# Joining two table products of a half group, with a new order of the pieces and new PSUM pair names, in a kernel of windowed attention beside a long convolution

## The chip, the core and the metric

The kernel runs on one core of one Trainium2 chip. The core has a matrix engine (PE, with its weight loads listed as PEld), a vector engine (DVE), a scalar engine (ACT), a general engine (POOL) and a queue engine (SP) that issues nearly all transfers (DMAs). Each engine works through its own instructions in the order in which the program emitted them; engines wait for each other by semaphores. PE writes only to PSUM, a small memory that DVE and ACT read.

The metric is device time in microseconds, from first to last instruction. Before the change the median of three runs is 782.46 us (779.48 to 783.68).

## What is computed

Two independent results are placed side by side, each 2048 x 576 numbers.

```
qkv = x @ wqkv                       # 2048 x 576 by 576 x 1728, 32 heads of 18
s   = q k^T / sqrt(18), keys 0..255 back only
a   = softmax(s) v, heads joined, @ wo

P   = exp(dt*A * l)                  # complex, per channel d, 128 states, l = 0..2047
K   = Re sum_n C_n P_n(l) dt*B_n     # the taps of a filter, 576 x 2048
b   = causal convolution of u with K, + u * Dskip
out = concat(a, b)
```

## The kernel before

**Four stages.** `front` loads weights and x and starts the projections. `tables` computes the projections q, k and v, the filter taps K and the first step of the transforms of u and K. `first` is short and ends the tables while attention starts. `rest` runs attention, the convolution in the transform domain, and at its end the product with wo. Attention works on 16 items (4 column blocks of 512 queries by 4 groups of 8 heads).

**The taps.** The 576 channels are 18 groups of 32, each two half groups of 16 channels. A half group c has a phase tile `fr` (sine and cosine, 128 x 2 x 512), an exponential table `mg` that stays in PSUM (128 x 1024), their products `Q` made by DVE in `t_q` (L595), and a table `m` made by POOL (`t_prod`, L579) and summed by DVE (`t_add`, L590). `t_taps` (L607) multiplies `m` and `Q` on PE.

**The order is written out by hand.** Each stage has a string in `PLAN` (L85). A letter is one step of a stream, and a letter with a digit is the next due follow-up of that kind of that stream. The emission order only fixes, for each engine, the order of its own instructions. Letters that matter here:

| letter | step | follow-ups |
|---|---|---|
| P | a third of a product of the projections, on PE (L417) | P1 P2 the high and low half of q and k, P5 v to SBUF, P4 P6 stores |
| G | angles of a group or a phase of a half group, on PE | G1 G2, G5 G6: ACT, then DVE |
| N, R | sine and A (ACT, POOL); product and sum (POOL, DVE) | |
| M | alternately `mg` on PE (M1: exp on ACT) and `t_q` on DVE | M1 |
| X | taps of a half group or transform of a group, on PE | X1 X5 ACT, X2 DVE, X4 store |
| U | first transform of u | U1 ACT, U2 DVE, U4 store |
| s | smax: scores of 64 queries for their row maximum, 16 to an item, then a transposition, on PE (L888) | s2: the maximum on DVE (L940), s6, s4 |
| a | score: one of 10 blocks of scores of an item, on PE (L962) | a1: exp on ACT (L1000) |
| v | pv: probabilities by v, 10 to an item, on PE (L1004) | v1: ACT |
| n | norm on DVE | n3 POOL, n1 ACT, n6 POOL, n4 the store of the item |
| c, d, e | spectra, inverse, last transform of the convolution, on PE | ACT, DVE, POOL, stores |
| f, k, L, y | loads by SP: convolution results, spectra, items, and the normed items for wo | |
| w | half of the product with wo for 128 rows, on PE (L1132) | w1 ACT, w4 store |

An item's row maxima go back into its Q tile by four small transfers (L933) before its first score step. The third item is loaded at the start of `first`, into memory that the projections leave.

**PSUM.** Three pairs of banks, called ring0 to ring2, serve all steps but the projections and pv. `SLOTS` (L134) names, one digit per tile, which pair each tile takes in the order of PE's steps. A step that takes a pair waits until the tile that had it before has been read by its follow-up. Projections have two banks of their own (`pp`), which pv (`po`) takes over.

**The end.** The wo product runs over 4 blocks c of 512 rows, 4 times 128 rows each, two halves h. `wo_in` (L1118) loads block c in two parts u of 256 rows with 8 transfers each, into the same tile for all c; part u of block c needs the stores of the items 4c to 4c+3 and waits for the wo steps that still read these columns.

Of the kernel before, what the change touches and what calls it, by code (L numbers as in the profile page):

```python
# [15 lines left out]
OP = mybir.AluOpType  # L16
# [13 lines left out]
HC = GC // 2  # L30
# [12 lines left out]
def constants():  # L43
# [23 lines left out]
    for nm, v in mult.items():  # L67
# [16 lines left out]

PLAN = {  # L85
    "front":
        "AAAVCACAAAAAVAVVV1CV1CAVAVAAVCAV1ACCVCACCVVV1VV1CVCACBBPABV1CCPV1BV1CPCPP1PVP2PP4CPAPP1PP2BPCP1P4BVP"
        "CP",
    "tables":
        "GMGPGPG5G6G1PM1GG5GP2G2PGG6P4NMMG5P1G6G5G1P2PPNM1PP4G6P1GPG2UNRP2G1MMRXPP1M1P2P4X1RMGG5NG2PRMPGP1G5X"  # L90
        "X1M1XG6X5GP2RG6PMX2RNRUPGU2PMG1UP1PG5G2M1RGNU1XXX1UG6P2MPX1G5U2RG6PX4MU1XP4RRPM1X4PXPGX5X2P1GNMUMP2P"
        "1PX1PG1RXP2M1P4PG2X1GP4PG5MUNRU1PG5G6MX4U2G6XP1U4RPRM1PPPGX5P4P2P1NMRGPP2MNXXX4G5X2G1P1P4PM1X1G6G2P4"
        "P2U4X1XMGPMGX5G5RP1PG6M1PP2X2PP4NRPP4RPMP1MG1PP2PM1UX4PP1XGRX1NP4XG2PP2GX1MG5UX4G5MPG6U2G6X4P4RU1U4R"
        "P1M1X4XX2PPXMRNU4P2GPX5P1X1MNRP2PXG1G2P4PGM1X1PG5PPXP5X4GPPP5RX5UMG5G6PG6UPPNU1UX2MRRPP4U2M1U4UU2XPP"
        "5MMRX1PGP5P6UG1U1PM1PPPG2P5UX4NRU1PMPMGM1XPP5PX1U2RU4G5P5GG5PPG6RMGXG6PP5PRX2NP6NP4PPG1MG2XPPGX5PRM1"
        "UP1G5P2P1MMGX1M1G5G6P2G6X4RXX4PPX1NXPPGP1X2PX5MGP4X4XG1RRP2MPX1PG5PNM1RG2G6XP1GX1PG5P1MMM1XG6X2P2X4P"
# [32 lines left out]
        "e4wewwn6w1e1yfww1wn4w1w4www1w4wwe4feeywe1w1ww4w4yw4wwe1we4w1ww1w4www1w4w1e4w4w4",
}  # L130

SLOTS = (  # L134
    "0122021210220122120112011211020210220101210201012021020012120012010210121000212102201221020110012201"
    "2011021012010201021120101201201201020201210210212012120210210120120021021102010212012212012012012012"
    "0120120210202021021021021020120120102102102020120120120121002102101202102012102102120121021201201201"
    "2012012010210210210210210210210120120120120120120120120120121021021012012012021021021021201201201201"
    "2101201201210210201210210210212012021020121020120120120210210210212010212012012012012021021012102102"
    "0102102102012012012010210210120120120210210201201201201210210201201201201201201201201201202102102101"  # L140
    "2012012010210210120120121021021021021021020120120120210120120102102102102102120120120120121200201201"
    "202010210210200210210212012"
)


# [9 lines left out]
class Kernel:  # L155
# [439 lines left out]
    def t_q(self, c):  # L595
        nc, tt = self.nc, self.nc.vector.tensor_tensor
        f = self.fr.pop(c)
        sn, cs = (f[:, i].rearrange("p (c m) -> p c m", m=32) for i in range(2))
        m = self.mg.pop(c)
        Q = self.Q[c] = self.p["Qp"].tile([128, HC, 2, 64], F32, name="Q")  # L600
        tt(Q[:, :, 0, 32:64], cs, m[:, :, 32:64], op=OP.mult)
        tt(Q[:, :, 0, 0:32], cs[:, :, ::-1], m[:, :, 0:32], op=OP.mult)
        tt(Q[:, :, 1, 32:64], sn, m[:, :, 32:64], op=OP.mult)
        nc.vector.scalar_tensor_tensor(Q[:, :, 1, 0:32], sn[:, :, ::-1], -1.0, m[:, :, 0:32],
                                       op0=OP.mult, op1=OP.mult)

# [666 lines left out]
```

## Time and profile before

| what | value |
|---|---|
| median of 3 runs | 782.46 us |
| all runs | 783.68, 779.48, 782.46 us |
| span of the profiled execution | 784.5 us (no other time of this execution is recorded) |
| mean granted clock of PE | 0.963 |
| instructions in the span | 29499 |
| moved by DMA | 150.67 MB |

The profile is one execution. Its page gives the busy time of each engine and the chain of work that ended last. Further views of the same trace group instructions by line, list the waits, cut the span into windows, or list instructions in order of time. In a row of the timeline the columns are start, duration, engine, line, operation, output and inputs, count, and in brackets the idle time before it with the engine and line that ended it. In a row of windows they are the length, the busy time of each engine with its count, then the granted clock of PE (1.00 is full), the DMA share and GB/s.

### The profile page before, as it was taken

The page shows a single profiled execution, that of the slowest core. Times are in us where ns is not written, and L with a number is a line of the kernel's source. Part 1 is how long each engine was busy: PE and PEld are TensorE (multiplying, and loading weights), DVE is VectorE, ACT ScalarE, POOL GpSimd, SP SyncE. Part 2 cuts the span into 40 slices and gives each one's busy share as a digit, 9 for nine tenths or more (in the row PEclk, how much of TensorE's full clock was granted, in tenths as well). Part 3 has the DMA queues.
Part 4 walks back from the last instruction along what each step waited for, and adds up shares of the span by engine and source line. Part 5 has one row for each costly group of instructions (what it writes and reads, how often), then busy time and mean ns, then how long its engine had stood idle before and what let it go on. Part 6 is the DMA issues. An engine that isn't in the chain of part 4 may idle for free.

```text
span 784.5 us, 29499 instructions
## 1 busy us (share of the span) xinstructions
PE 693.0 (88%) x12956; PEld 410.8 (52%) x12956; DVE 588.2 (75%) x779; ACT 534.3 (68%) x709; POOL 417.3 (53%) x309
## 2 busy tenths in 40 slices
PE   3786878998989989997789999989989998999997
PEld 2532444565545654665544555544555554557775
DVE  5998789998998897988777888876888586852100
ACT  2369577787887777773458677775877876786622
POOL 2245867987688666866007574451553444546120
PEclk9979799999999999996999999998999999899999
DMA  8998055738247537889578777676866786555786
GB/s 309 342 215 204 7 133 149 159 83 216 51 120 182 133 70 175 230 183 277 113 238 279 247 240 231 207 243 166 245 185 203 240 256 207 170 163 159 205 258 187
DMA packets 215904, 150.67 MB, mean 192 GB/s; under 512 B 103530, under 2 KB 195818, under 8 KB 215520
## 3 DMA queue, kind: packets, MB, share of 16 engines
q1 hardware_dynamic: 214160, 146.28, 66.0%
q0 software_dynamic: 1616, 2.52, 1.1%
q8 instruction: 101, 1.65, 0.8%
q14 instruction: 27, 0.22, 0.1%
HBM read 83.50 MB, written 65.11 MB: 189 GB/s over the span
## 4 chain that ended last, share of the span: by engine, by line
PE 55%; DVE 17%; ACT 15%; issue 6%; DMA 4%; SPq 1%; POOL 0%; ACTq 0%; DVEq 0%
PE po L1020 9%; PE pp L204 9%; PE ring L204 7%; PE ring L906 5%; DVE m L940 5%; PE ring L752 4%; PE ring L982 4%; PE ring L615 4%; PE ring L718 4%; PE ring L505 2%; DMA wraw<-in_wr_dram 2%; DVE amx L192 2%; PE ring L815 2%; ACT raw L1000 2%; DVE wl L372 2%
## 5 line engine op out<-in xcount | busy, mean ns | idle before, releaser
L940 DVE TENSOR_REDUCE m<-ring 128x2 f32<-128x640 f32 (+4 forms) x256 | 190.8, 779 | 66.0 <-PE ring L914 58.2
L586 POOL TENSOR_TENSOR m<-A,tr 128x1024 f32<-128x1024 f32 x72 | 141.5, 1983 | 52.6 <-DVE m L592 43.5
L1000 ACT ACTIVATE P<-ring,esc 128x1024 f32<-128x1024 f32 (+2 forms) x86 | 90.0, 1060 | 37.1 <-PE ring L995 32.7
L1000 ACT ACTIVATE raw<-ring,esc 128x1024 f32<-128x1024 f32 (+2 forms) x74 | 77.2, 1061 | 19.4 <-PE ring L995 18.8
L734 POOL TENSOR_TENSOR t<-X 128x768 f32<-128x768 f32 x24 | 46.7, 1944 | 76.1 <-ACT X L726 75.6
L1063 POOL TENSOR_TENSOR oh<-osb,oh 128x1024 f16<-128x1024 f32 x16 | 34.1, 2133 | 59.5 <-ACT oh L1059 42.9
L914 PE MATMUL ring<-sm,idb 64*64 64x128 bf16 x896 | 56.1, 224 | 3.3 <-issue 3.1
L204 PE MATMUL pp<-xh,wh 128*128 128x512 f16 x180 | 48.1, 397 | 10.0 <-DVE qst L453 5.0
L204 PEld LDWEIGHTS <-wh 128*128 128x128 f16 x324 | 30.7, 99 | 49.1 <-issue 11.7
L615 PE MATMUL ring<-Q,m 128*32 128x64 f32 x2304 | 42.9, 231 | 12.8 <-ACT fa L511 4.1
L1055 POOL TENSOR_TENSOR osb<-osb,T 128x1024 f32<-128x1024 f32 x16 | 38.6, 2410 | 25.8 <-DVE T L1050 23.8
L592 DVE TENSOR_TENSOR m<-m,m 128x1024 f32<-128x1024 f32 x36 | 51.6, 1432 | 0.7 <-POOL m L586 0.6
L615 PEld LDWEIGHTS ring<-Q,m 128*32 128x32 f32 x2304 | 36.9, 117 | 27.2 <-ACT mab L547 5.5
L906 PEld LDWEIGHTS <-raw 54*64 54x64 f16 x704 | 28.6, 108 | 41.1 <-issue 37.7
L740 POOL TENSOR_TENSOR Y<-t,t 128x384 f32<-128x384 f32 x24 | 24.7, 1029 | 46.1 <-DVE t L734 33.8
L906 PE MATMUL ring<-K,raw 54*64 54x320 f16 (+4 forms) x576 | 44.8, 308 | 4.5 <-ACT raw L1000 0.8
L204 PE MATMUL pp<-xh,wl 128*128 128x512 f16 x180 | 48.0, 400 | 0.6 <-DVE wl L372 0.6
L567 POOL TENSOR_TENSOR tr<-tr,mab 128x768 f32<-128x768 f32 x18 | 33.3, 1850 | 28.4 <-ACT tr L562 28.4
L726 ACT ACTIVATE X<-ring 128x768 f32<-128x768 f32 x48 | 36.7, 812 | 14.3 <-PE ring L718 8.1
L995 PE MATMUL ring<-tm,idb 64*64 64x256 bf16 (+2 forms) x640 | 45.0, 257 | 0.0
L982 PEld LDWEIGHTS <-K 55*64 55x64 f16 x1280 | 28.8, 108 | 26.7 <-issue 22.7
L752 PE MATMUL ring<-Y,i 32*64 32x192 f32 x768 | 38.7, 336 | 3.3 <-issue 2.3
(171 smaller groups left out, 1725.1 us busy)
## 6 DMA issues: line engine op xcount, KB each, us to landing
gk<-kst SPq DMA_DIRECT2D x36, 256.0 KB
gx<-ust SPq DMA_DIRECT2D x16, 576.0 KB
xk<-gx SPq DMA_DIRECT2D x24, 384.0 KB
xk<-gk SPq DMA_DIRECT2D x24, 384.0 KB
h<-ho SPq DMA_DIRECT2D x48, 192.0 KB
hp<-h SPq DMA_DIRECT2D x24, 384.0 KB
K<-kz SPq DMA_DIRECT2D x14, 512.0 KB
raw<-qz SPq DMA_DIRECT2D x11, 512.0 KB
```

The costliest lines, as they stand in the source:

```text
L204: self.nc.tensor.matmul(ps, u, v, start=(i == 0), stop=(i == len(ops) - 1))
L586: tt(m[part], A[:, ch, a0:a0 + 8].unsqueeze(3).to_broadcast(sh), tr[:, ch, part, 0:8].unsqueeze(2).to_broadcast(sh), op=OP.mult)
L592: self.nc.vector.tensor_tensor(m[0], m[0], m[1], op=OP.add)
L615: nc.tensor.matmul(kp[32 * st:32 * st + 32, j, :], m[:, ch, 32 * term:32 * term + 32], Q[:, ch, term, :], start=(term == 0), stop=(term == ...
L734: mul(ts[i], X[:, :, :, :192].rearrange("p i s j -> p s i j"), X[:, i, :, 192:].unsqueeze(2).to_broadcast(sh), op=OP.mult)
L752: nc.tensor.matmul(ps[64 * (b % 2):64 * (b % 2) + 64, b // 2, 192 * s:192 * s + 192], self.i1[32 * b:32 * b + 32, t, o:o + 64], Y[32 * b:3 ...
L906: nc.tensor.matmul(ps[z:z + 64, b, :n], d["Q"][rr, 2 * b + pp, 64 * qb:64 * qb + 64], d["K"][rr, 2 * b + pp, k0:k1], start=True, stop=Fals ...
L914: nc.tensor.matmul(out, self.idb[rr], self.sm[rr], start=False, stop=True, skip_group_check=True)
L940: self.nc.vector.tensor_reduce(out, x, axis=AX.X, op=OP.max)
L982: nc.tensor.matmul(ps[z:z + 64, b, off:off + w], d["K"][rr, 2 * b + pp, kc:kc + 64], d["Q"][rr, 2 * b + pp, q0:q0 + w], start=(k == 0), st ...
L1000: nc.scalar.activation(P[:, :, lo:hi], ps[:, :, lo:hi], AF.Exp, scale=self.esc)
L1020: nc.tensor.matmul(po[32 * p:32 * p + 32, z, q0:q0 + w], V[64 * z:64 * z + 64, kb * 76 + 19 * p:kb * 76 + 19 * p + 32], P[p % 2][64 * z:64 ...
```

## The change

In `t_q` two products of `mg[32:64]`, with cosine and with sine, become one instruction. It reads the sine and cosine tiles in reversed order as one operand of 16 x 2 x 32 elements and repeats the table along that middle dimension. The number of elements written is the same. The other two products keep their own instructions.

```
-        tt(Q[:, :, 0, 32:64], cs, m[:, :, 32:64], op=OP.mult)
+        tt(Q[:, :, :, 32:64], f.rearrange("p i (c m) -> p c i m", m=32)[:, :, ::-1],
+           m[:, :, 32:64].unsqueeze(2).to_broadcast([128, HC, 2, 32]), op=OP.mult)
         tt(Q[:, :, 0, 0:32], cs[:, :, ::-1], m[:, :, 0:32], op=OP.mult)
-        tt(Q[:, :, 1, 32:64], sn, m[:, :, 32:64], op=OP.mult)
         nc.vector.scalar_tensor_tensor(Q[:, :, 1, 0:32], sn[:, :, ::-1], -1.0, m[:, :, 0:32],
                                        op0=OP.mult, op1=OP.mult)
```

All strings of `PLAN` and `SLOTS` are replaced. Every step and follow-up occurs as often as before in the whole program, and `front` differs in two places (the store of the constant rows goes before two stores of q on SP, and the high half of the third projection product goes behind the last conversion of weights on ACT). The start of `tables`, the string `first` and the end of `rest`:

```
     "tables":
-        "GMGPGPG5G6G1PM1GG5GP2G2PGG6P4NMMG5P1G6G5G1P2PPNM1PP4G6P1GPG2UNRP2G1MMRXPP1M1P2P4X1RMGG5NG2PRMPGP1G5X"
+        "GGG1G2PP1P2P2P4ZMM1G5G6GPPG5GG6P4NMPNRGGG5G6GG5G6G1PP1P2P4PPPPG2NURRMM1MG1P1P2PMG2GG5XG6M1RX1MMM1XGN"
...
     "first":
-        "s6X5s4sX2s2sX4s2RMsss2M1saaRs2Xa1ssa1s2X1MRXs2X1sXX4saas2aX5sas2sX2X4sa1sa1s2vX4s2vs2a1ss2X4s2s2ss2s"
-        "s2aavsa1sssa1s",
+        "Xss2s2X1XX5X2aa1ss2sas2ss2aaa1a1sss2s2a1vsss2vs2vaa1sss6sss2ss2s2s2ss2aaa1sa1s2vsaa1s2ss2ss2X4X4",
...
-        "e4wewwn6w1e1yfww1wn4w1w4www1w4wwe4feeywe1w1ww4w4yw4wwe1we4w1ww1w4www1w4w1e4w4w4",
+        "e1ywww1www4w4ee4yww1w4ww1www1w4w4www1e1e4e4www4w1w4",
```

Counted from the strings, with the steps on PE behind `front` numbered from 0 (1014 in both):

| PE step | number before | number after |
|---|---|---|
| first taps | 18 | 21 |
| first smax of item 0 | 323 | 309 |
| last projection step | 320 | 348 |
| last transform of K (end of the tables) | 355 | 354 |
| first score of item 0 | 348 | 355 |
| first smax of item 2 | 374 | 371 |
| first spectra | 405 | 401 |
| last pv | 990 | 990 |

The number of PE steps from a tile to the next tile in the same pair, counted over all tiles of a stage:

| stage | 1 or 2 steps, before | after | 3 steps, before | after |
|---|---|---|---|---|
| tables | 32 | 42 | 42 | 32 |
| first | 10 | 6 | 16 | 16 |
| rest | 46 | 63 | 144 | 128 |

Two neighbouring PE steps of one kind in `rest`: smax behind smax 42 times before and 57 after, score behind score 19 and 34, score behind smax or smax behind score 161 and 123.

Behind the last pv, PE has the same steps in both orders: 12 wo halves and 3 last transforms, then the 8 wo halves of block 3. On SP, the second part of block 2 (8 loads) and one convolution load stand ahead of the store of the last item in both. Before the change one output store of wo and one of the convolution (two transfers) stand ahead of these 8 loads, behind the store of item 14; after it none does. On ACT, item 14's conversion to half precision moves behind item 15's copy out of PSUM, and item 15's conversion stands behind two wo outputs there instead of one.

More of the change, by code (lines that the diff above doesn't have):

```diff
@@ L92 @@
[L92 to L96, printed above, removed]
@@ new lines @@
+        "4PX5P4P1MP4P4MM1PP2GP1X2G5X4X4PPG6NUU1RP2U2X4PPU4PP4P4MMGRRP1P2G1M1PU4G2XX1PGG5P1XP4X1MG6GG5PPP1MM1P"
+        "2PNG6NRXX5RP2PPPP1X2XX4X4X4PMMP2X1P4RPRM1PP5UMUU2PPUU1P5PXX1GGG5G6GG5PG6PG1G2P5PPNPPPPRRXNX2XX5U4X4X"
+        "1UP5U1MRUM1U2P5URU1U2PPPMGP5MG1PU4U4M1XPX1G2GG5MPPGPG6G5G6PPNP5RP5XRX5MP6GP6P6PPPM1NG1RX2PPXX1RPMMP1"
+        "P4G2P1P4P2P4P2GXM1X1MPPX4G5G6GG5G6NRRMRPX4XX2PM1PPUP1P2MNXPX5MP1X1P2GG1M1GPP4RP4G2PP1XX1PP6GMG5G5G6G"
+        "6P2XMX4X2X5M1NRRNPPP1UU2P4P4MUPP2XX1PRRU1UX4U2GPMG1G2U1M1MMXM1P1P2PX1GG5X4G6NX4RGG5PG6PPRMXNP4X2UPPX"
@@ new lines @@
+        "5P1P1UP2GG1RPPU4U1P4U2PRP5UMM1X4X4P2G2XP4XX1X1MNGPG5G6MPPM1GP5PPG5PG6NP6XPP5RPRZZX2X5PXX1PPX4PRP5GG1"
+        "PMNGPG5P4MRPP5PG2RPM1PP5PG6P5GXPMG5G6X1XX2PUPX5U4U2P6MP5U1RRRP6UP6GM1NPPPP1G1PPXX1U4PMMG2XM1X1UP2PU1"
+        "NP1MGG5X4U2MX4X4GPPP2PM1PPG6G5G6XRRNMP1RP4P4P1XP2X5U4X1GG1X2UUU1RPU2MP2M1PGPG2XMP1P2G5P4X1GMG6G5G6X4"
+        "PX4M1PNP4RRMPPXX2NP1X5P2ZRRGU4XX1X4X4G1PMZPG2PPP1P2P4GM1P4MG5NGG5G6G6RPRP1PUUMU1XU2RPPP2M1X1NNXMX2PR"
+        "UPX5UP1XU4U1U2GUG1P2G2PMPM1P5X1X4PPUMU4U1U4U2U4GGG5G5P5G6PG6PRRMP6M1XMX4P4PPPX1XX5PX4X2sss2ss2sss2s2"
@@ L129 @@
[L129 removed]
+        "vaa1ssss2vs2avss2s2vs4aa1a1aa1ksvss2kaa1ss2s2cc1sLLss6svv1s2sss2s2lsss2s2s2c2aa1svvsc6s2c3sks2kcs2ss"
+        "2c1aava1alkskka1a1Laa1lvcs2c6vvc2nc1aa1aa1svvs4aa1dc3d1c2ss2n3s2sc6vvs2ksaaLs2v1a1Lda1Lnad1a1sc3vcc1"
+        "c6n3s2ss6sas2ss2a1aa1ss2vsass2a1s2vksaas4a1s2a1sava1s2ss2aa1svvs2ss2aaaa1a1ss2vac2c3svvks2a1a1aa1sss"
+        "2s2n1n6cc1sds2sc2LLLvd4v1dd1s2ss6kLssd4d1svs2s2c6c3s2kcc1sc6s2dsd4s2avd1a1ss2aa1aa1c2ssn1n6s2s2vvaa1"
@@ new lines @@
+        "ss2ss2s4sks2kcc1savvc3c6ss2s2a1aa1c2c3kdd4d1savvkss2s2a1aa1d4aLa1dd1Lnvss2vv1n4cc1sLLLd4s6asc2aa1a1v"
+        "kss2s2ss2ks4kan3va1ss2ss2sss2aa1svs2s2sasa1s2s2vn4vssd4s2s2aa1n1ss2c6c3vsss2ss2s2css6Lc1Laac6avva1a1"
+        "a1Lssvaa1ns2vss2as2sa1s2sn6v1dss2s2vc2vss2ad1a1sn3aa1s2aa1c3sn1s2vals4avvn4a1vnsn3svs2s2n6a1ss2kcc1k"
+        "kss2aa1c6ad4ss2vaaa1sls2a1a1vvLLfc2aa1sffeLs2c3ss6Le1e4fkkaa1sss2ss2s2csv1c1c6vs4ss2s2sas2vvsss2s2a1"
+        "n1dsss2d1vs2Lsas2da1anc2d1slva1avLLs2aa1a1svs2ss2asLvvs2a1ala1saa1s2n3sss6kvn4s2ss2sn6v1cs2c1sls2ala"
@@ new lines @@
+        "1vsaa1s2ss2vn1sass2s2ss2vlkss2a1ss2llaa1vad4ffa1see1svs2s2ss4ass2s2a1Lc3c2vaa1kc6n6cc1dc3dd4d1d1snaa"
+        "1LLLvs2ss6ss2vsssn4vvv1s2ss2s2s2d4aa1ss2as4vss2ya1aa1vasvss2s2aa1a1aa1vsn3ss2vss2s2aa1ee1kc2ss2ss2va"
+        "nn1ca1c6c1avkn4saLa1ss2a1as2a1vss6aac3c6LLLn6svs2vkkLa1a1ssas2s2skv1vn3s2c2a1avsa1ss2cc1as2da1asnvd1"
+        "vsc3s2c6n4c2c3n3s4a1asla1s2lvs2sssvvn1n6s2s2LLsaa1s2s2ss2e4e4aa1ss2avss2La1ala1vvv1sss6ssks2s2aa1s2v"
+        "aa1d4sksvvs2s2sssn1s2Lan6n4s2a1vsvss2s2s2aca1s4svc1c6aa1svs2aa1s2fsfdsd1s2s2ac2asvs2a1ss2d4vva1ss6aa"
@@ new lines @@
+        "v1a1LLdLa1nd1lsas2vss2aa1a1vssss2s2s2ac3a1vss2scc1s2ss2aaka1va1sn3nd4s2ydd1d4ee1ss2sc2vvs4avn1a1s2ss"
+        "2kc6kLLsn4s2cc1Lss2vass2a1aka1n6aa1ss2vvc3Lss6ac2a1ss2dd1n3ss2v1d4sss2s2c6cc1ss2avsaa1sks2s2vffaka1a"
+        "1aa1kn1c3svc2ss2vsfs2s2see1aa1s2ss2dss2ss2e4ld1vn6cc6c3c1lss4ass2s2vaann3a1a1a1d4LLfLc2aa1vess6n4vLs"
+        "d4e1aa1s2ss2llvvsdv1vad1a1s2ss2kcss2vd4c6c1sss2c3s2dd1aasla1va1c2ss2ks2vssks2c6c3ls2kcc1ac6a1ss2kvvs"
+        "n1s2aa1cc2c3vc1c6sss2dsd1s2s2fdsls6s4ad4d1kfe4a1waaa1a1d4ww1wwaaLw1vd4a1a1c2c3kcvc1n6vaaa1w4wwa1aaff"
@@ L143 @@
+    "0120102102102102102120102102102012010210210210201201201202102120120120210210201201201201201201201202"
+    "1021021021201021021021021021020120121021021012012102102102102102120120121021021021201012012012012012"
+    "102102102102102102101021010"
 )
```

52 lines of the change are left out of this document (13 added, 39 removed).

## The prediction

> **What bounds the kernel now.** I read the engines' busy time and the chain's shares on the page first, then a table of windows that cuts the span where its character changes.
>
> ```profile
> PE 693.0 (88%) x12956; PEld 410.8 (52%) x12956; DVE 588.2 (75%) x779; ACT 534.3 (68%) x709; POOL 417.3 (53%) x309
> PE 55%; DVE 17%; ACT 15%; issue 6%; DMA 4%; SPq 1%; POOL 0%; ACTq 0%; DVEq 0%
> 0.00:60.00 60.00, 38.03 (x142) 20.87 (x143) 49.17 (x53) 24.20 (x32) 17.34 (x22) 0.91 0.91 287
> 60.00:100.00 40.00, 30.15 (x247) 14.57 (x247) 32.55 (x47) 30.96 (x49) 29.41 (x25) 0.83 0.46 109
> 100.00:355.00 255.00, 231.84 (x3233) 137.64 (x3231) 225.47 (x307) 198.62 (x319) 190.79 (x148) 0.99 0.60 145
> 355.00:405.00 50.00, 38.27 (x985) 26.18 (x989) 40.85 (x66) 20.62 (x29) 13.71 (x13) 0.83 0.75 209
> 405.00:700.00 295.00, 274.87 (x7280) 154.16 (x7272) 228.62 (x296) 222.82 (x241) 143.21 (x92) 0.98 0.73 221
> 700.00:784.50 84.50, 79.79 (x1082) 57.39 (x1080) 11.51 (x14) 37.04 (x44) 22.88 (x13) 1.00 0.64 196
> ```
>
> The chain is mostly PE, with DVE and ACT in turns: no one engine is late, they hand PSUM pairs to each other. In the tables (100 to 355) PE has 91% and DVE 88%, so DVE time saved there can show. In attention with the convolution (405 to 700) PE has 93%, 20.1 us idle in all, and DVE 77%. The loosest place is the transition, 355 to 405: PE is idle for 11.7 of 50 us and its clock is 0.83. The end is PE alone.
>
> **Joined product.** Two instructions of 512 elements become one of 1024, 36 times.
>
> ```profile
> L601 DVE TENSOR_TENSOR Q<-fr,ring 128x512 f32<-128x512 f32 x36 | 24.5, 680 | 7.6 <-ACT ring L527 4.9 <-PE ring L615 2.0 <-ACT fr L557 0.7
> L603 DVE TENSOR_TENSOR Q<-fr,ring 128x512 f32<-128x512 f32 x36 | 24.4, 679 | 0.0
> 350.35 0.68 DVE L602 TENSOR_TENSOR Q<-fr,ring 128x512 f32<-128x512 f32 x1
> 350.94 0.68 DVE L603 TENSOR_TENSOR Q<-fr,ring 128x512 f32<-128x512 f32 x1
> 351.54 0.67 DVE L604 SCALAR_TENSOR_TENSOR Q<-fr,ring 128x512 f32<-128x512 f32 x1
> 353.19 1.22 DVE L592 TENSOR_TENSOR m<-m,m 128x1024 f32<-128x1024 f32 x1
> 354.33 0.68 DVE L514 TENSOR_TENSOR fr<-ring,fr 128x512 f32<-128x512 f32 x1
> ```
>
> Each lasts 0.68 us, but the next starts 0.60 us on (350.35, 350.94, 351.54). A product of 1024 lasts 1.22 us and the next starts after 1.14. By starts the pair falls from 1.20 to 1.14, 0.06 x 36 = 2.2 us; by durations from 1.36 to 1.22, 0.14 x 36 = 5.0 us. The trace has no product with a repeated, reversed operand of this shape; a loss is excluded by L602, which reads reversed at the same 0.68, and by the means of 679 and 680 ns over 36, which show that this PSUM operand meets no contention. So 0 to 5.0. I take the starts, nearest to what a queue without gaps pays, times DVE's 88%: **-2 us**.
>
> [...]
>
> **The start of the tables.** Here PE waits longest, 4.12 us for the first taps.
>
> ```profile
> 78.01 1.94 PE L615 MATMUL ring<-Q,m 128*32 128x64 f32 x64 [4.12 <-ACT fa L511]
> ```
>
> The new order has two more projection thirds ahead of these taps, but also one more low half of q (0.6 us of DVE by the start spacing) ahead of the first phases, on which sine, POOL's product and the taps hang. What is filled is work moved up, what is late is the chain: 0, with -2 and +1 as bounds.
>
> **The transition.** Before, all projections end first and then smax of item 0 runs as a block, with DVE's maxima behind it.
>
> ```profile
> 340.00:345.00 5.00, 4.12 (x84) 2.73 (x85) 1.89 (x3) 4.67 (x9) 3.74 (x5) 1.00 0.78 170
> 360.00:365.00 5.00, 3.82 (x80) 2.67 (x80) 4.92 (x12) 0.18 (x1) 4.76 (x7) 0.50 0.92 216
> 365.00:370.00 5.00, 4.42 (x102) 3.14 (x103) 4.35 (x6) 0.06 (x1) 3.08 (x4) 0.50 0.98 375
> 353.63 0.65 PE L204 MATMUL pp<-wh,xl 128*128 128x288 f16 x4
> 361.51 7.83 DVE L940 TENSOR_REDUCE m<-ring 128x2 f32<-128x128 f32 x14
> 361.65 0.32 PE L906 MATMUL ring<-raw 54*64 54x128 f16 x4 [1.10 <-DVE Q L604]
> 365.21 0.68 SPq L882 DMA_DIRECT2D V<-vd  x1
> Q<-qz SPq DMA_DIRECT2D x5, 512.0 KB
> 393.61 0.22 PE L906 MATMUL ring<-K,Q 54*64 54x64 f16 x4
> ```
>
> DVE has 3.1 us free in 340 to 345 and is full at 361.51, where 14 maxima take 7.83 us while ACT does nothing. The new order starts smax 14 steps earlier and ends the projections 28 steps later, so maxima and projections run beside each other. What can be won is bounded by DVE: its idle 9.15 us of 355 to 405. Against it stands the third item's load. It needs memory of the projections, so it goes out behind the last of them. Before, it was issued by 365.89 and wanted at 393.61, 27.7 us later; the new order leaves 23 PE steps instead of 54. Three transfers of at most 0.5 MB each at the stage's 209 GB/s are 7 us and their issues 2 (3 x 0.68); 23 steps of maxima at 0.56 us are 13. It fits, and where it does not, smax waits in PE's queue and all scores behind it. I put that at up to 4. So -9 to +4, and I take a third of the gain: **-3 us**.
>
> **The pairs of PSUM in `rest`.** This speaks against the change.
>
> ```profile
> L940 DVE TENSOR_REDUCE m<-ring 128x2 f32<-128x640 f32 x224 | 176.4, 821 | 60.0 <-PE ring L914 58.2
> L1000 ACT ACTIVATE P<-ring,esc 128x1024 f32<-128x1024 f32 x72 | 79.4, 1114 | 27.0 <-PE ring L995 26.4
> 443.59 0.33 PE L906 MATMUL ring<-K,raw 54*64 54x320 f16 x4 [0.32 <-ACT ho L759]
> 443.87 0.33 PE L906 MATMUL ring<-K,raw 54*64 54x320 f16 x4
> 458.71 0.33 PE L982 MATMUL ring<-raw,K 55*64 55x320 f16 x4 [0.26 <-ACT P L1000]
> ```
>
> A smax occupies PE for 0.28 us (443.59 to 443.87), its maximum DVE for 0.82, an exp ACT for 1.11. A pair named again with one step between leaves PE short by about 0.8 us where that step is a smax (1.11 less 0.33), with two by 0.45. One-step cases go from 46 to 63, two-step cases from 144 to 128: +13.6 and -7.2, a net 6.4 us if all were of this kind. On the same scale the order before would lose 37 + 65 = 102, while PE's measured idle is 20.1, a fifth: many of these steps are long. Behind the wait stand all further smax, score and pv steps in PE's queue, and so DVE and ACT. Between a fifth (1.3) and all (6.4) I take **+3 us**, since scores and smax now come in blocks (164 like neighbours against 122) and DVE idles while ACT has a block.
>
> **The end.**
>
> ```profile
> 737.37 3.24 PE po L1020 x121
> 749.01 13.35 PE ring L204 x108
> 763.12 3.33 DMA oh<-od
> 767.21 13.40 PE ring L204 x108
> 748.78 2.12 POOL L1063 TENSOR_TENSOR oh<-osb,oh 128x1024 f16<-128x1024 f32 x1 [1.49 <-ACT oh L1059]
> 755.15 1.48 SPq L1068 DMA_DIRECT2D od<-oh  x4
> 760.65 0.93 SPq L1129 DMA_DIRECT2D oh<-od  x1
> 762.77 2.86 PE L815 MATMUL ring<-hp,i 128*64 128x384 f32 x16
> ```
>
> Item 15 is ready at 750.90, its store goes out at 755.15, its loads from 760.65; PE ends its other work at 765.63 and waits until 767.21, 1.58 us. In the new order two stores less stand before, ACT's two moves cost item 15 0.6 us, and its 8 loads wait for two wo rows of block 2 (4 halves of 1.68) behind 4 others and two transforms: 740.61 + 6.7 + 2.9 + 6.7 = 756.9, 3.7 before 760.65. The wait goes, and PE alone is late next, with the same steps: **-1.5 us** (0 if the store still goes out as late).
>
> **Sum.** -2 - 3 + 0 + 3 - 1.5 = -3.5 on 784.5, 781.0 for the profiled execution. That one lies 2.04 over the median of 782.46; I keep the difference: **779.0 us**.
>
> **Rivals.**
>
> *A full transition.* All 9 us of DVE's idle go, the pairs cost 1.3 instead of 3, the rest as summed: -2 - 9 + 1.3 - 1.5 = -11.2, 771. For it: at 360 to 370 PE is busy 8.24 us at clock 0.50, so filled gaps would also double its pace (up to 4 us of PE time). Against it: DVE is full there. [...]
>
> *Pairs asked for too soon (the other side).* All 6.4 us in `rest`, and the same in the tables, where cases of one step or none go from 32 to 42.
>
> ```profile
> L511 ACT ACTIVATE fr<-ring 128x512 int32<-128x512 f32 x36 | 21.5, 598 | 11.9 <-PE ring L505 9.4 <-POOL wi L338 1.7 <-DVE Q L604 0.6
> ```
>
> A phase tile holds its pair for 0.60 on ACT and 0.68 on DVE; ten such cases cost up to 10 x 1.28 less 5 for a step between, some 8. With the transition at nothing: -2 + 6.4 + 8 - 1.5 = +10.9, 793. It decides when the extra waits pass the 6.5 us of gains; in the tables DVE, not PE, would have to be left without work.
>
> *The change does nothing that counts.* DVE waits 7.6 us ahead of L601 anyway, so the saved 2.2 end as longer waits, and order against order cancels: 782.5, within 2.
>
> **Chances.** 0.5% is 3.9 us, about what a measurement of this kernel can tell from no change: 778.5 and 786.4 are the bounds. The forecast (775.5 to 782.5) 0.45, of it 0.18 below the bound; full transition (768 to 776) 0.25; pairs (785 to 796) 0.25, of it 0.04 within; nothing 0.05. Faster 0.43, same 0.36, slower 0.21. The range leaves out the ends of both rivals: 770 to 791. The likeliest case's own range is 775.5 to 782.5.
>
> **What would show it.** Right: L601 at some 1.22 us, DVE 2 to 5 us less busy; maxima from L940 beside projections, and less PE idle than 11.7 us where smax of items 0 and 1 runs; attention with somewhat more PE idle than 20.1 us; no DMA wait ahead of the last 13.4 us. Wrong: smax of item 2 waiting for its load, idle PE in the tables behind L511 or L514, or clock dips at new places.

## The result, and the profile after

| | before | after |
|---|---|---|
| median of the runs side by side, us | 783.07 (779.48 to 786.34) | 792.68 (788.60 to 796.93) |
| span of the profiled execution | 784.5 | 791.2 |

The ratio of the times is 1.0138, with a 95% interval from 1.0093 to 1.0183: the change costs 7 to 14 us. 779.0 was forecast, with 770 to 791 as the range. A median here and below is over all runs of a kernel, while a ratio leaves out runs more than 1.5% above the kernel's fastest, so that for e4, e5 and e6 the two don't quite match.

The page of the changed kernel, first the busy time of the engines, then the shares of the chain:

```profile
PE 691.7 (87%) x12956; PEld 403.3 (51%) x12956; DVE 581.9 (74%) x743; ACT 533.2 (67%) x709; POOL 417.4 (53%) x309
PE 45%; DVE 22%; DMA 11%; ACT 11%; issue 6%; SPq 3%; POOL 1%; DVEq 0%; ACTq 0%
```

DVE works 6.3 us less and no engine works noticeably more, and yet the span is 6.7 us longer. In the chain PE falls from 55 to 45%, while DMA rises from 4 to 11% and SP's queue from 1 to 3%. Time is lost in waits, and transfers are among them. But a transfer can stand on the chain with its whole length where PE waited for its last part alone: the load `K<-kz` takes 7.08 us of the chain from 402.11 on, and PE waits 0.34 us for it.

The table of windows, with the same columns as before and the same cuts:

```profile
0.00:60.00 60.00, 37.78 (x143) 20.96 (x144) 49.12 (x54) 23.07 (x30) 16.21 (x22) 0.94 0.95 297
60.00:100.00 40.00, 29.92 (x232) 13.51 (x231) 29.92 (x38) 28.20 (x44) 23.64 (x20) 0.70 0.35 88
100.00:355.00 255.00, 227.16 (x3181) 133.08 (x3180) 225.17 (x279) 197.70 (x317) 196.42 (x152) 0.99 0.60 145
355.00:405.00 50.00, 41.17 (x1021) 26.56 (x1027) 38.94 (x63) 23.35 (x35) 15.38 (x13) 0.94 0.83 205
405.00:700.00 295.00, 269.09 (x7102) 146.98 (x7087) 226.37 (x299) 214.96 (x233) 139.30 (x90) 0.98 0.70 214
700.00:791.20 91.20, 86.61 (x1293) 62.23 (x1290) 12.41 (x14) 45.97 (x53) 26.47 (x14) 1.00 0.69 208
```

Three rows differ. From 60 to 100 PE's clock is 0.70 instead of 0.83. From 355 to 405 PE idles 8.8 us instead of 11.7 and runs at 0.94 instead of 0.83: the transition became denser, as meant. From 405 to 700 PE idles 25.9 us instead of 20.1, and 1293 matmuls instead of 1082 are left at 700.

**The joined product,** from the groups by line with shapes kept apart:

```profile
L601 DVE TENSOR_TENSOR Q<-fr,ring 128x1024 f32<-128x1024 f32 x36 | 43.6, 1212 | 4.9 <-ACT ring L527 4.1 <-ACT fr L557 0.8
L603 DVE TENSOR_TENSOR Q<-fr,ring 128x512 f32<-128x512 f32 x36 | 24.4, 677 | 0.0
```

One instruction of 1212 ns stands for two of 680, as forecast. For the 36 pairs the rows give 24.5 + 24.4 - 43.6 = 5.3 us of DVE, where the prediction's durations gave 5.0. That this would shorten the kernel the runs below don't show.

**The start of the tables.** The timeline of PE, the first taps; then SP's queue and one row of ACT ahead of them:

```profile
87.42 1.93 PE L615 MATMUL ring<-Q,m 128*32 128x64 f32 x64 [0.55 <-DVE fa L514]
```
```profile
48.21 3.25 SPq L412 DMA_DIRECT2D kz<-ones  x1
51.55 2.48 SPq L466 DMA_DIRECT2D qz<-qst  x1
54.13 2.26 SPq L467 DMA_DIRECT2D qz<-qst  x1
56.44 2.41 SPq L466 DMA_DIRECT2D qz<-qst  x1
58.90 2.56 SPq L467 DMA_DIRECT2D qz<-qst  x1
```
```profile
64.89 0.60 ACT L450 ACTIVATE qst<-pp 128x512 f16<-128x512 f32 x1 [6.70 <-DMA qz<-qst]
```

The first taps start at 87.42 instead of 78.01. The store of the constant rows (L412, 2 x 1280 KB) now goes out ahead of the first stores of q. Behind it the next four issues take SP over 2 us each, where these stores of q took 0.31 to 0.39 before. The staging tile of q comes free late, ACT stands 6.70 us in front of it, and the sines behind it in ACT's queue (L556) start at 68.71 instead of 62.58.

**The start of attention.** SP's queue and one row of PE:

```profile
385.59 5.62 SPq L639 DMA_DIRECT2D gk<-kst  x2
391.32 2.07 SPq L776 DMA_DIRECT2D w<-in_c_w_dram  x1
393.58 0.82 SPq L776 DMA_DIRECT2D i<-in_c_i_dram  x2
394.50 2.49 SPq L933 DMA_DIRECT2D raw<-m  x4
397.10 0.53 SPq L706 DMA_DIRECT2D xk<-gx  x1
```
```profile
402.14 1.08 PE L982 MATMUL ring<-raw 55*64 55x64 f16 x8 [3.16 <-DMA raw<-m]
```

The row maxima of item 1 go back into its Q tile at 394.50, behind the last stores of K's transform and 2 MB of constants; they land when PE has waited 3.16 us for them. Before, the only wait of a score step for such a store, in the whole execution, is one of 0.4 us:

```profile
PE ring L982 <- DMA raw<-m: 0.4, 1, 0.4
```

**The end.** The last pieces of the chain:

```profile
744.56 3.27 PE po L1020 x118
747.82 6.97 PE ring L204 x56
754.79 2.73 PE ring L815 x16
757.52 13.83 PE ring L204 x112
771.35 1.44 PE ring L815 x8
772.79 11.93 PE ring L204 x97
```

No transfer stands ahead of the last block any more: the 1.58 us of before are gone. PE wasn't idle for all of them. Two rows of its timeline before, at the start of this block:

```profile
766.49 0.42 PE L204 MATMUL ring<-woh,oh 128*128 128x288 f16 x2 [0.51 <-DMA oh<-od]
767.21 0.28 PE L204 MATMUL ring<-woh,oh 128*128 128x288 f16 x1 [0.30 <-issue]
```

Its idle time there was 0.81 us, 0.51 of it for the load; in the rest it worked on four matmuls of the block. From the last pv's end to the span's end it is 43.4 us instead of 43.9.

### The profile page after: what moved, and what is told of

The parts are those of the page before. It is cut to its first block, busy times and chain, and to the rows that moved or that the text cites. A ratio compares the mean times of both kernels' runs of the same rounds, so it can differ in the third digit from the quotient of the medians.

```text
span 791.2 us, 29495 instructions
## 1 busy us (share of the span) xinstructions
PE 691.7 (87%) x12956; PEld 403.3 (51%) x12956; DVE 581.9 (74%) x743; ACT 533.2 (67%) x709; POOL 417.4 (53%) x309
## 4 chain that ended last, share of the span: by engine, by line
PE 45%; DVE 22%; DMA 11%; ACT 11%; issue 6%; SPq 3%; POOL 1%; DVEq 0%; ACTq 0%
PE ring L204 7%; PE po L1020 7%; PE pp L204 6%; DVE m L940 5%; PE ring L752 4%; PE ring L982 4%; PE ring L906 4%; PE ring L718 3%; DMA K<-kz 3%; DVE m L592 3%; DVE Q L601 2%; PE ring L815 2%; DMA wraw<-in_wr_dram 2%; DVE amx L192 2%; PE ring L505 2%
## 5 line engine op out<-in xcount | busy, mean ns | idle before, releaser
L940 DVE TENSOR_REDUCE m<-ring 128x2 f32<-128x640 f32 (+4 forms) x256 | 190.1, 779 | 67.7 <-PE ring L914 64.6
L592 DVE TENSOR_TENSOR m<-m,m 128x1024 f32<-128x1024 f32 x36 | 53.7, 1492 | 5.5 <-POOL m L586 5.4
L914 PE MATMUL ring<-sm,idb 64*64 64x128 bf16 x896 | 53.5, 220 | 4.4 <-issue 4.4
L615 PE MATMUL ring<-Q,m 128*32 128x64 f32 x2304 | 41.1, 226 | 8.1 <-DVE Q L604 2.6
L726 ACT ACTIVATE X<-ring 128x768 f32<-128x768 f32 x48 | 36.7, 809 | 16.9 <-PE ring L718 11.7
L601 DVE TENSOR_TENSOR Q<-fr,ring 128x1024 f32<-128x1024 f32 x36 | 43.6, 1212 | 4.9 <-ACT ring L527 4.1
L615 PEld LDWEIGHTS ring<-Q,m 128*32 128x32 f32 x2304 | 35.4, 113 | 21.1 <-issue 6.6
L906 PEld LDWEIGHTS <-raw 54*64 54x64 f16 x704 | 25.7, 106 | 39.9 <-issue 36.1
```

The source lines that it names most:

```text
L592: self.nc.vector.tensor_tensor(m[0], m[0], m[1], op=OP.add)
L601: tt(Q[:, :, :, 32:64], f.rearrange("p i (c m) -> p c i m", m=32)[:, :, ::-1], m[:, :, 32:64].unsqueeze(2).to_broadcast([128, HC, 2, 32]), ...
L615: nc.tensor.matmul(kp[32 * st:32 * st + 32, j, :], m[:, ch, 32 * term:32 * term + 32], Q[:, ch, term, :], start=(term == 0), stop=(term == ...
L906: nc.tensor.matmul(ps[z:z + 64, b, :n], d["Q"][rr, 2 * b + pp, 64 * qb:64 * qb + 64], d["K"][rr, 2 * b + pp, k0:k1], start=True, stop=Fals ...
L914: nc.tensor.matmul(out, self.idb[rr], self.sm[rr], start=False, stop=True, skip_group_check=True)
L940: self.nc.vector.tensor_reduce(out, x, axis=AX.X, op=OP.max)
```

## The experiments

Theories were A (the front costs the time), B and later C (the order inside attention does), D (the tables and the transition do, later D2, in e8 called E: the transfers at the start of attention), F (the names of the pairs), G (blocks of smax steps wait for DVE's maxima), H (the order of the engines' steps, whatever the resource) and I (transfers in general). A gain or loss below is the ratio to the kernel before times 782.5 us, with its 95% interval; the change itself stands at +10.8 (7.3 to 14.3).

**The parts that are easily parted: front and product.** e1 and e2 exchange one string (below for e1; for e2 it is the other way round), e3 and e4 the product, by the diff of the change above.

```
     "front":
-        "AAACVAAACAAAVAACVV1CV1VAVAAAACVV1AVV1CVCVCV1VCCCAPCCBBV1VVBCAACV1V1VVPBCCPPPP1PP2P4CPPP1P2P4PBCCBPP1"
-        "PP",
+        "AAAVCACAAAAAVAVVV1CV1CAVAVAAVCAV1ACCVCACCVVV1VV1CVCACBBPABV1CCPV1BV1CPCPP1PVP2PP4CPAPP1PP2BPCP1P4BVP"
+        "CP",
```

> The changed kernel with the stage string front of the kernel before: the store of the constant rows goes behind the first two stores of q again, and the high half of the third projection product goes ahead of the last weight conversion. Theory A (the front costs the time): ACT's wait of 6.7 us for a q staging tile goes, the first taps start at 78 to 80 us instead of 87.4, and the total falls by 5 to 9 us against the changed kernel, to 784 to 788. Theory B (the order in attention costs the time): the first taps come as early, but the tables are bound by PE and DVE and no more than 2 us of it reach the end; the total stays at 790 to 793.

> The kernel before with the stage string front of the changed one, nothing else. Theory A (the front costs the time): first taps at 84 to 88 us instead of 78.0 and a total of 788 to 792, 5 to 9 us over the kernel before. Theory B (attention costs it): first taps late by some us, total within 2 us of the kernel before.

> The kernel before with the joined product alone, old order and old pairs. By the forecast: one instruction of 1.21 us in 36 places for two, DVE 5 to 6 us less busy, total 2 us less (0 to 5), 778 to 783. If DVE's saved time only lengthens its waits: within 1 us of the kernel before.

> The changed kernel with the two products apart as before: new order and new pairs alone. By the forecast 2 us more than the changed kernel (0 to 5), 793 to 797. If DVE's time in the tables is not what sets their end: within 1 us of the changed kernel.

| | time, us | against before |
|---|---|---|
| e1, new with old front | 792.11 | +8.8 (5.2 to 12.4) |
| e2, old with new front | 780.95 | -1.4 (-3.8 to +1.0) |
| e3, old with joined product | 781.52 | -0.1 (-2.7 to +2.6) |
| e4, new with two products | 797.85 | +11.7 (7.1 to 16.3) |

In e1 the timeline shows the first taps early again:

```profile
81.06 1.93 PE L615 MATMUL ring<-Q,m 128*32 128x64 f32 x64 [0.55 <-DVE fa L514]
```

6.4 us earlier, and the time doesn't follow. Theory A falls. In e2 the new front alone leaves the first taps at 78.15: it takes the new order of the tables behind it to make the late store felt. The other 3 us of the delay (81.06 against 78.01) come with the new order of the tables whatever the front. The joined product brings nothing that these runs can tell from no change: its 2 us lie within e3's interval, and e4's lies over the change's, but overlaps it.

**Splices.** The two orders hold the same steps, so one can be followed up to a point and then what is left be done in the other's order, with the other's pairs. The code of the change is kept throughout. The first lines that differ in e6, where the old order takes over at the start of `rest`:

```
-        "vaa1ssss2vs2avss2s2vs4aa1a1aa1ksvss2kaa1ss2s2cc1sLLss6svv1s2sss2s2lsss2s2s2c2aa1svvsc6s2c3sks2kcs2ss"
+        "as4a1vakLsvssksvLvksa1sks2vvv1as2ala1s2s2s2sas2s2aa1svcvsaa1a1as6snsasvc1cac6a1s4s2ss2va1ks2a1kLas2c"
...
```

> The changed kernel's code with the order of before up to the end of the stage first, and from there the pieces that are left in the new order with their new pairs. Theory C (the order inside attention costs the time): 788 to 793, as the changed kernel. Theory D (the loss lies in the tables and the transition): 779 to 784, as the kernel before.

> The reverse: the new order up to the end of the stage first, then the pieces that are left in the old order with their old pairs. Theory C (attention's order costs the time): the forecast's gain of the transition shows, 776 to 782. Theory D (tables and transition): 787 to 793.

> The new order up to score step 6 of item 6, somewhat under half of attention, then the old order. If the loss falls at one place at the start of attention (late transfers of item 1's maxima and of item 3's load at 394 to 409 us): 788 to 793, the whole loss. If it accrues with the pairs over all of attention: about half of it, 784 to 787. If it comes late: 778 to 783.

> The new order up to score step 4 of item 2 (some 430 us), then the old order with its pairs: the new order's start of attention alone, with its transfers of 394 to 410 us. Theory D2 (the transfers at the start of attention cost most): 789 to 794. Theory G (the many short waits between 410 and 545 us): 783 to 788, as the run that changed back at the start of the stage rest (786.2).

> The old order up to score step 6 of item 6, then the new order with its pairs: the reverse of e7. If all of the loss lies in the first part of attention, as e7 (whole loss) says: 778 to 783. If the second part costs as well: 785 to 790.

| | time, us | against before |
|---|---|---|
| e5, old, new from `rest` on | 793.49 | +9.8 (2.3 to 17.2) |
| e6, new, old from `rest` on | 786.22 | +4.1 (1.0 to 7.3) |
| e12, new to some 430 us, then old | 790.92 | +8.1 (5.2 to 11.0) |
| e7, new to item 6, then old | 794.73 | +14.3 (9.9 to 18.6) |
| e16, old to item 6, then new | 793.67 | +13.0 (8.8 to 17.1) |

e5 and e6 part the change at this boundary: most of it goes with the new `rest`, as C had it (788 to 793), while e6 falls between the forecasts of C (776 to 782) and D (787 to 793). The two intervals are wide, but the profiles of the kernels with the same piece of order agree; times of the first and last row of taps (L615) and of the span, in us:

```
order of tables / rest   kernel   first taps  last taps  span    last taps to end
old / old                before     78.0       381.1     784.5   403.4
old / old                e2         78.2       382.2     782.9   400.7
old / old                e3         78.9       381.3     780.9   399.6
new / old                e6         88.0       383.2     781.4   398.2
old / new                e5         78.5       381.3     792.9   411.6
new / new                after      87.4       380.2     791.2   411.0
new / new                e1         81.1       377.7     790.0   412.3
new / new                e4         88.3       383.5     792.4   408.9
```

With the old order of `rest` it is 398 to 403 us from the last taps to the end, with the new one 409 to 412, whatever the tables were. So some 10 us are lost in `rest`. The tables, 9.5 us late at the first taps, have nearly caught up at the last ones: over the profiles of all kernels here the mean of the last taps is 381.3 in the old order of the tables (8) and 382.8 in the new one (12), with single ones from 377.7 to 389.5.

The splices in the middle didn't locate the loss further. e12 came out as D2 had it (789 to 794), but e7 and e16 lie above all that was expected of them (at most 793 and 790): each half alone costs as much as the whole, which can't add up. An explanation that no run tests is that a splice there costs something of its own, since steps that the other order had ahead are missing from the mix; e5 and e6 are spliced where both orders start the stage.

**The transfers at the start of attention.** e8 moves one step, the store of item 1's maxima; e13 does that and breaks up the load of the constants, e14 and e15 only the latter, in e3 and e6. First the edit of e8, then that of the constants, whose other pieces go out behind the loads of spectra 0 to 2.

```
     "first":
-        "Xss2s2X1XX5X2aa1ss2sas2ss2aaa1a1sss2s2a1vsss2vs2vaa1sss6sss2ss2s2s2ss2aaa1sa1s2vsaa1s2ss2ss2X4X4",
+        "Xss2s2X1XX5X2aa1ss2sas2ss2aaa1a1sss2s2a1vsss2vs2vaa1sss6sss2ss2s2s2ss2aaa1sa1s2vsaa1s2ss2ss2s4X4X4",
     "rest":
-        "vaa1ssss2vs2avss2s2vs4aa1a1aa1ksvss2kaa1ss2s2cc1sLLss6svv1s2sss2s2lsss2s2s2c2aa1svvsc6s2c3sks2kcs2ss"
+        "vaa1ssss2vs2avss2s2vaa1a1aa1ksvss2kaa1ss2s2cc1sLLss6svv1s2sss2s2lsss2s2s2c2aa1svvsc6s2c3sks2kcs2ss"
```
```
     def conv_setup(self):
-        for n in ("w2", "i1", "i2"):
-            nc.sync.dma_start(getattr(self, n), a["c_" + n])
+        nc.sync.dma_start(self.w2[:, 0:1], a["c_w2"][:, 0:1])
     def conv_load(self, n):
...
+        if n == 0:
+            nc.sync.dma_start(self.w2[:, 1:4], a["c_w2"][:, 1:4])
...
```

> The changed kernel with one step moved: the store of item 1's row maxima (four transfers) goes out ahead of the last two stores of the transform of K instead of behind them and behind the three loads of constants. In the changed kernel score step 0 of item 1 waits 3.16 us for it on PE. Theory E (late transfers at the start of attention cost a good part): that wait goes, 2 to 4 us less than the changed kernel, 788 to 790. Theory C (the many short waits on pairs): PE waits elsewhere, within 1 us of the changed kernel, 791 to 794.

> The changed kernel with the start of attention relieved: item 1's maxima are stored ahead of the last stores of K's transform (as in e8), and of the convolution's three tables of constants (2 MB, loaded in one go ahead of the first spectra) only the first eighth of one goes out there, the rest in pieces behind the loads of spectra 0 to 2. Theory D2 (transfers at the start of attention): both waits of PE (3.2 us for the maxima, or 6.5 us for the spectra in e8) fall under 1 us and 3 to 6 us come back, 787 to 790. Theory H (the order of steps inside attention, many short waits): within 2 us of the changed kernel, 791 to 795.

> The kernel before with the joined product and the constants in pieces in the same way. In the order of before PE's waits for transfers at the start of attention are under 1.5 us in all, so 779 to 782, 0 to 2 us under the kernel before by either theory.

> The new order up to the end of the stage first, then the old one (as e6, 786.2), with the constants in pieces. If e6's 4 us over the kernel before are the transfers that the new order sends later there: 780 to 783. If they are PE and DVE work of the transition: 784 to 788.

e8 took 796.49 us (+16.7, 12.2 to 21.3), e13 795.13 (+13.8, 10.1 to 17.7). The lists of PE's waits, first e8's, then e13's:

```profile
PE ring L718 <- DMA xk<-gk: 6.5, 1, 6.5
```
```profile
PE ring L727 <- DMA xk<-gk: 3.1, 1, 3.1
```

The wait for the maxima is gone in both, and the first spectra wait for their load in its place. What is issued sooner on SP made what stands behind it later: in the three orders tried here PE waits 3.2, 6.5 and 3.1 us for a transfer of this place. So neither repair took the wait away, and neither gained anything; e8 came out above both its forecasts (788 to 790 and 791 to 794), e13 at the upper end of H's (791 to 795). That D2 isn't the main cause rests on the size of the wait, 3.2 of some 10 us, and on PE's idle time behind 410 us, below. That breaking up the constants would cost nothing was a miss: e14 took 786.67 (+4.5, 1.6 to 7.4), where e3 had -0.1, and why isn't shown. e15 took 786.32 (+5.1, 2.7 to 7.5), as e6, but with such a cost of the repair itself it doesn't tell what e6's 4 us are.

**The names of the pairs.** e9 keeps the new order and names only the pairs of `rest` again. One line of `SLOTS` from there:

```
-    "0210210210210210212012012012101201201201201201201201201201201201201210210210210210210210210212012012"
+    "1201201201201201202102102012010210201201201201201201201201201201201021021021021021021021012012012012"
...
```

> The changed kernel with all steps in the new order and only the pairs of the stage rest named again: each tile takes, of the pairs whose last reader stands ahead, the one that was given out longest ago. Cases with one or two steps between a tile and the next in its pair fall from 63 to 50, those with three rise from 128 to 140 (before: 46 and 144). Theory F (the names cost the time): most of the 10 us comes back, 782 to 787. Theory G (the order of the steps costs it, whatever the names): within 2 us of the changed kernel, 790 to 795.

815.46 us, +32.2 (27.1 to 37.2), far outside both forecasts: 21 us more than the change, though fewer cases have one or two steps between them. The largest of e9's waits on PE between 405 and 745 us that end with DVE or ACT:

```profile
PE ring L981 <- ACT X L725: 3.5, 6, 0.9
```

The spectra hold two pairs while ACT copies them (L726, two copies of 0.81 us in turn), and the rule of e9 gives such a pair out when its turn comes. The count of steps between two tiles in a pair, on which the prediction worked out its price, is thus no measure; when the reader ends, is. Worked out from the rows of DVE and ACT (the end of each tile's reader, in order), between 410 and 700 us the named pair came free later than another one in 13 of some 420 tiles before the change, by under 3 us in all; in 15 to 19 after it, depending on how a step's start is taken, by under 3 us as well; in e9 in some 45, by over 16. So by this measure the names of the change are as good as those before, and F falls.

**The length of the maxima.**

```
-                self.post("2", (ps,), lambda out=mv[:, :, 8 * pp + qb], x=ps[:, :, :n]: self.red(out, x))
+                self.post("2", (ps,), lambda out=mv[:, :, 8 * pp + qb], x=ps[:, :, :n // 2]: self.red(out, x))
```

> The changed kernel with row maxima taken over the first half of each block's keys only: some 250 maxima of 0.82 us on DVE become about half as long. Theory G (smax steps in blocks wait for DVE's maxima): the new order loses what set it apart, 779 to 785, and its excess over the old order with the same cut falls to under 4 us. Theory D2 (late transfers at the start of attention): the excess over the old order with the same cut stays at 8 to 12 us.

> The kernel before with the same cut: row maxima over the first half of each block's keys only. It is the base for the run above. PE has 6 us or so of waits behind maxima and 20 us of idle time in attention, so 772 to 780, 3 to 10 us under the kernel before.

In both the mean maximum of L940 between 405 and 745 us falls to 484 ns, from 808 in the changed kernel and 809 in the one before. e10 took 791.73 us (+11.1, 6.2 to 16.1), e11 777.18 (-4.6, -6.5 to -2.7). The old order gains some 4 us, the new one no more than the runs can tell, and the distance between them grows to about 15, above what either theory had (under 4, 8 to 12). G falls: it isn't the time that DVE takes for a maximum.

**Fewer transfers.**

```
     def conv_load(self, n):
+        if n >= 2:
+            self.cl[n] = self.x2[n % 2]
...
         def store(ho):
-            for s in range(2):
-                nc.sync.dma_start(v[t, s], ho[:, s])
             self.n["h"] += 1
...
     def hload(self):
-        hv = self.h.rearrange("f a l j -> (f a) l j")
+        hv = self.gx.rearrange("f a l j -> (f a) l j")
```

> The changed kernel with about a third of the transfers of attention left out: the convolution's spectra 2 to 23 reuse the loads of spectra 0 and 1 (17 MB less), and its results aren't stored, but read back from the transform of u (9 MB less). All work of the engines stays. Theory I (transfers cost the new order its time: late loads, and PE's stops inside a step, 9 to 13 us in the new order against 4 to 9 in the old, that stand where the DMA engines are full): the excess over the old order with the same cut falls to 0 to 4 us, and the stops to under 4 us in both. Theory H (the order of the engines' steps): the excess stays at 8 to 12 us.

> The base for the run above: the old order with the joined product (as e3, 781.5 us) and the same transfers left out. By theory I the old order gains less than the new one, 0 to 5 us, 776 to 782; by theory H as much as the new one, 0 to 10.

e17 took 788.93 us (+6.5, 3.6 to 9.4), e18 773.29 (-8.5, -12.4 to -4.5). The excess of the new order over the old is 15.6 us, not less: theory I falls as the main cause, and H is left, though it had 8 to 12. By the two profiles 11.1 us of the excess stand behind the last taps (399.1 against 388.0 us to the end), and the others ahead of them (389.5 against 383.4). Windows of attention behind its start, e17 and then e18:

```profile
410.00:550.00 140.00, 128.38 (x3425) 71.44 (x3429) 111.05 (x146) 103.36 (x115) 70.61 (x45) 0.98 0.46 141
550.00:745.00 195.00, 186.19 (x4719) 109.05 (x4705) 125.12 (x164) 145.75 (x157) 88.78 (x56) 1.00 0.48 142
```
```profile
410.00:550.00 140.00, 132.23 (x3568) 74.51 (x3552) 113.53 (x153) 106.42 (x120) 76.00 (x49) 1.00 0.46 141
550.00:745.00 195.00, 188.91 (x4553) 116.88 (x4540) 121.58 (x154) 142.89 (x153) 90.31 (x55) 1.00 0.49 147
```

With the DMA engines busy less than half the time PE idles 20.4 us in the new order and 13.9 in the old one. Some 1.5 us of the difference still belong to a transfer, the store of item 1's maxima, which in e17 comes late again:

```profile
411.45 1.17 PE L986 MATMUL ring<-raw 55*64 55x64 f16 x12 [3.17 <-DMA raw<-m]
```

The rest is no wait of PE for a transfer.

**Where PE idles.** The same windows of the changed kernel and of e3 (which differs from the kernel before by the product alone):

```profile
410.00:550.00 140.00, 127.53 (x3423) 70.66 (x3419) 113.29 (x154) 103.17 (x114) 72.47 (x46) 1.00 0.71 218
550.00:745.00 195.00, 182.42 (x4471) 106.20 (x4473) 120.01 (x151) 139.99 (x150) 86.53 (x55) 0.97 0.68 206
```
```profile
410.00:550.00 140.00, 131.09 (x3506) 74.25 (x3503) 112.64 (x152) 105.06 (x118) 75.97 (x49) 1.00 0.75 229
550.00:745.00 195.00, 186.59 (x4512) 112.70 (x4505) 122.64 (x154) 141.29 (x150) 88.19 (x54) 0.98 0.69 209
```

25.1 us against 17.3, in both halves. From the lists of PE's waits between 405 and 745 us, summed by what ended them (us; "stops" are those that end with nothing the list of waits shows; the last section tells what they have in common):

```
kernel     idle 410 to 745   DVE and ACT, count   transfers   stops, count
before        19.1              8.6, 30              0.0        9.2, 11
e2            16.8              9.2, 34              2.0        3.6, 5
e3            17.3              9.0, 33              2.7        4.3, 7
after         25.1             12.3, 41              1.2        9.8, 12
e1            27.6             11.5, 39              1.3       13.2, 12
e4            24.8             10.4, 36              3.7       11.0, 10
e18 (old)     13.9              9.7, 34              0.4        1.8, 4
e17 (new)     20.4             14.1, 48              3.2        2.7, 4
```

On the mean of three each, the new order idles 8.1 us more: 2.5 of it behind DVE and ACT, 5.6 in stops. The stops differ much between executions (before and after, taken alone, have 9.2 and 9.8), but three more of each say the same: with e6, e14 and e15 the old order has 6.1 us of stops and 8.9 behind DVE and ACT on the mean, with e5, e8 and e13 the new one 11.1 and 11.0. Where transfers are left out the stops nearly go, in both orders, and yet the new one takes 11.1 us more behind the last taps; of its 6.5 us more of idle time 4.4 are waits on DVE and ACT. So the stops are where a good part of the loss shows, but without them it remains.

## Why the prediction was wrong

*The joined product, -2:* the mechanism is right, 1212 ns and DVE 6.3 us less busy. The size isn't shown: e3 has -0.1 with -2.7 to +2.6, in which the -2 lies too. In the one profile of e3 nothing of it arrives, though DVE has 88% in the tables: the last taps start at 381.3, as before (381.1).

*The start of the tables, 0 with +1 as the bound:* wrong. The first taps came 9.4 us late, 6.4 of them because of a store on SP and a staging tile that the step didn't look at: it counted the steps of PE and DVE and left the two moves in the front unpriced. Two of the prediction's own signs of being wrong came true here, PE idle behind L514 (3.2 us in two waits between 55 and 105 us) and a clock dip at a new place (0.70 between 60 and 100 us). The tables regained nearly all of it, so this cost little in the end.

*The transition, -3:* right in the window, wrong for the whole. PE idles 8.8 instead of 11.7 us there, at clock 0.94 instead of 0.83. From 360 to 370, where the clock was 0.50 with PE busy for 8.24 us, it is 1.00 with 9.30. But all of the new order ahead of `rest`, which the forecast put at -2 - 3 + 0 = -5, gave +4.1 (1.0 to 7.3) in e6; where these 9 us went stays open, and e6's one profile (span 781.4) doesn't show them. The doubt about the third item's load was put at the wrong transfer: that one was in time. What came late was the small store of item 1's maxima; 3.16 us, within the 4 that stood as the bound.

*The pairs in `rest`, +3 with 6.4 as the upper bound:* this is the step that failed, since it was the only price put on 340 us of a new order. PE's waits on DVE and ACT grew by 2.5 us, close to the +3; `rest` as a whole lost some 10, against +3 - 1.5 in the forecast. The reasoning by distances fell with e9, which has fewer short distances and is 21 us slower. (Its 164 like neighbours against 122 aren't those of smax and score alone, which have 57 + 34 = 91 against 61.) The stops, 5.6 us of the rise, stood in the profile of before as waits that end with "issue", and the prediction passed them over.

*The end, -1.5:* the wait went as described; of the 1.58 us 0.5 show. The prediction read the whole of 765.63 to 767.21 as waiting, where PE was idle for 0.81.

Of the rivals, "pairs asked for too soon" named 793 and the right sign. Its terms don't hold: 8 us were to come from pairs in the tables, which regained time, and the names weigh as little after the change as before.

What in the order of `rest` makes PE wait stays open. Shown is that it lies there (e5, e6), and that it isn't the names (e9 and the ends of the readers), the length of DVE's maxima (e10, e11) or the third of the transfers that e17 and e18 leave out. The transfers at its start have a part of some 3 us that no run took away. That blocks of like steps leave one of DVE and ACT idle while PE waits for the other is in accord with the waits on DVE and ACT, which grew, but no run took the blocks apart. None of the versions was faster than the kernel before by more than the runs can tell, save those that leave work out.

## What to carry to other kernels

A hand-written order is priced by what each queue does with it, SP's among them: one store of 2 x 1280 KB moved ahead of small ones delayed a tile, ACT by 6.70 us and the first taps by 6.4, and one of 4 x 2 KB behind constants held PE for 3.16. A delay early in a stage with slack, or a gain in one window, says little about the end; two orders of the same steps can be spliced at a stage boundary, and two such runs, with their profiles, say which stage pays. A transfer put right at a crowded place here made the next one late (a wait of 3.2 us became one of 6.5 or 3.1), so the place has to be counted as a whole.

## What the runs showed of the hardware that was not expected

**PE stops inside a step.** A row of PE's timeline in the changed kernel, four matmuls of one smax step whose operands are the same:

```profile
524.03 0.22 PE L914 MATMUL ring<-sm,idb 64*64 64x128 bf16 x3
525.35 0.24 PE L914 MATMUL ring<-sm,idb 64*64 64x128 bf16 x1 [1.10 <-issue]
```

The fourth comes 1.10 us after the third, with no semaphore between them. In attention such stops take 3.6 to 13.2 us in all, the longest 2.32 us in the kernel before and 1.71 in the changed one; with a third of the transfers left out they take 2.7 (new order) and 1.8 (old). So they shrink with the traffic. But not all of them stand where the DMA engines are full, as theory I had it: from 413.66 to 415.83, up to the end of one stop of the changed kernel, the DMA share is 0.09, from 600.55 to 603.56, up to the end of another, 1.08, and from 405 to 745 it is 0.70. The page lists a DMA queue for instructions:

```profile
q8 instruction: 101, 1.65, 0.9%
```

That is 16.3 KB to a packet. The 25,912 instructions of PE and its weight loads on the same page would be 257 to a packet, as an estimate, if all the packets were PE's.

Counted through PE's records in order (matmuls, weight loads and its sequencer's), each of the 12 stops of the changed kernel between 405 and 745 us stands ahead of a record whose number, from 0, leaves 193 when divided by 256. Each ends 1.26 to 1.44 us after a packet of this queue has ended, of which there are 63 in these 340 us. In the kernel before it is the same remainder for all 11 stops, 1.26 to 1.64 us behind a packet, with 64 packets. So in both traces the stops stand whole multiples of 256 records apart, close to the 257 of the estimate. That they are blocks of instructions that reach PE late is the author's reading of this pattern; no row shows what a packet holds. Nor does a run show why a packet would come late, beyond the fall of the stops with fewer transfers.

**SP slows behind a large store.** Behind the store of the constant rows four issues took SP 2.26 to 2.56 us each, where the same stores took 0.31 to 0.39 ahead of it in the kernel before. There the slow issues are others, again those behind the store. Rows of SP's queue before the change:

```profile
51.30 0.39 SPq L467 DMA_DIRECT2D qz<-qst  x1
55.21 0.46 SPq L412 DMA_DIRECT2D kz<-ones  x1
55.72 2.17 SPq L1198 DMA_DIRECT2D wk<-in_c_wk_dram  x1
57.93 2.40 SPq L1200 DMA_DIRECT2D dsk<-in_dsk_dram  x1
```

What makes them slow no run shows.
